# A gated FFT mixer and squared-ReLU MLP, forward and backward: loads of one queue moved to another, and the work around them reordered

## The chip, the cores and the metric

One NeuronCore of a Trainium2 chip. The metric is device time in microseconds (us) of the whole kernel, from its first instruction to its last; the median of three runs is given. A profile is one further execution, taken by the hardware profiler. Its span is a little shorter than the time of the same execution, because something lies before the first and after the last recorded instruction.

The engines, as the profile names them: PE is the matrix engine (PEld its weight loads), DVE the vector engine, ACT the scalar engine, POOL the GpSimd engine, SP the sync engine, which here only issues DMAs. A "q" behind an engine's name (SPq, ACTq) is its sequencer: it waits and issues, while the engine itself may be busy.

## What is computed

The forward function and all its gradients, from a given gradient of the output:

```python
def _A_ref(x, w_r, w_i):                       # x: 1 x 2048 x 1024
    X = rfft2(x.astype(float32), axes=(-2, -1))
    X = X * (w_r + 1j * w_i)                   # w: 2048 x 513
    return irfft2(X, s=(S, D), axes=(-2, -1)).astype(bfloat16)

def _B_ref(x, w1, b1, w2, b2):                 # w1: 1024 x 3584, w2: 3584 x 1024
    h = einsum("bsd,df->bsf", x, w1) + b1
    r = where(h > 0, h, 0)
    return einsum("bsf,fd->bsd", r * r, w2) + b2

g = sigmoid((x * gate_w).sum(-1, keepdims=True))
out = g * _A_ref(x, A_w_r, A_w_i) + (1 - g) * _B_ref(x, B_w1, B_b1, B_w2, B_b2)
# returned: out, and the gradients of x, w_r, w_i, w1, b1, w2, b2, gate_w
```

## The kernel before

The kernel has three stages, one behind the other on PE, and a Fourier transform that runs beside the first two.

**First pass of the MLP** (`mlp_in`, to about 462 us). It computes the hidden layer (`ph`, L740 and L847) and the gradient of the hidden layer (`pd`, L747; DVE makes `dhT` of it on L751), and stores both, transposed, to DRAM (`h2T_scr`, `dhT_scr`). Features go in pairs of 128 (`fp`, 0 to 13), rows in halves (`sp`). A `Unit` is one pair and one half: seven chains of four matmuls (`p1` to `p7`) in place of eight, by Strassen's scheme; between them stand four `back_` steps of the unit before, eight matmuls each. PSUM banks are few: `ph` has two, and `pd` shares two with `pZ`. A `pd` chain starts when DVE has read the bank two chains back. The X bank is copied by ACT (`cu`, `u2`, L851) and then accumulated into again. The sums of rows that the scheme needs lie in the tile `dbn`, whose own contents (gradient rows) have been saved to `db_scr` and are loaded again by `again` (L1001).

**Second pass** (`mlp_grads`, about 462 to 860 us): the gradients of w2 and w1, by `Block`s of seven chains of eight matmuls (L1143). A group of 512 features comes back from DRAM through transposing DMAs (`turned`, L183; four of them make a group) into `even` or `odd` in turn. DVE makes the scheme's sums (`total`, L1075) from these groups and from `dbn`.

**Third pass** (`Outputs`, from about 860 us): the two large outputs.

**The transform.** `fft_mid` is a generator of 32 turns (`turns`: 16 frequency pairs `m`, two halves `h`). A turn loads `z` (two DMAs of 128 KB, L393), adds and subtracts (`mirrored`, L413 and L414), multiplies on PE (`px`, L422), copies to `x` on ACT (L423; an edge column from `ex` on L424), multiplies with the filter on DVE (`products`, L430 and L431), joins to `y` (`joined`, L436 to L442), multiplies back (`pv`, L450; `pc`, L456 and L457), and computes the filter's gradient (`grads_of_w`, L467 to L471). `spread` deals the steps of the transform between the steps of the MLP at a fixed rate, in the first pass 1.5 steps for each step of the MLP. A turn is four steps. The first `px` is at 235.4 us and the last at 595.4 us; their distance repeats as 6.4, 12 and 12 us.

Each engine runs its instructions in the order in which they were recorded. `after(..., NoSync)` fixes an order alone; with `Sync` it is a wait. All hardware-issued DMAs share eight completion semaphores in turn, so a DMA also waits for the landing of the one that used its semaphore last.

SP issues, in one order: the loads of w1 (L769), the transposed loads of w2 and of the groups (L183), the loads of `z` (L393) and of `dbn` (L1001). The two lines that issue what the change moves:

```python
ld(out=z[:, n], in_=columns_of(z_scr, c, h))                       # L393, inputs
after(turned(grp[n][:, k * KH : (k + 1) * KH, f_], in_), later["blocks"])   # fetch
```

In the last units the order of pairs and halves is (11,0), (11,1), (12,0), (12,1), (13,1). The half 0 of pair 13 is done without the scheme, at the very end of the pass (`more`), with `forth` and `back_` in turn and then four `back_` alone.

Of the kernel before, what the change touches and what calls it, by code (L numbers as in the profile page):

```python
# [141 lines left out]
def kernel(  # L142
# [22 lines left out]
    nc = tc.nc  # L165
# [40 lines left out]
    nc.scalar.dma_start(out=identb[:], in_=cten["identb"].ap())  # L206
    kf = pers.tile([P, 2, P], FDT, name="kf", tag="kf")
    flip = pers.tile([P, 1], FP32, name="flip", tag="flip")
# [25 lines left out]
    def columns_of(scr, c, h):  # L234
        return scr[:].rearrange("t c r x h l -> c h (r x) t l")[c, h]
# [89 lines left out]
    def fft_mid(filler):  # L325
        fb, fbs = pool("f2", "right")
        NM, G = R1 // 2, nc.gpsimd
        WL = HW + 2
# [4 lines left out]
        def edges():  # L333

            ed = fb.tile([P, NM, 2, 4], FDT, name="ed", tag="ed")
            low = fb.tile([P, NM, 4], FDT, name="low", tag="low")
            mid = fb.tile([P, 4], FDT, name="mid", tag="mid")
# [19 lines left out]
        def edges_through(ams, ed, low, mid):  # L357
# [8 lines left out]
            for h in range(2):  # L366
                for m in range(NM // 2):
                    for n in range(2):
# [3 lines left out]
                        )  # L372
            ex = fb.tile([P, NM, 2, 2, 2], FDT, name="ex", tag="ex")
            for n in range(2):
                for c in range(2):
                    nc.vector.tensor_copy(
                        out=ex[lanes[n], :, c], in_=sp[lanes[c], :, n, :].rearrange("p m (e t) -> p m t e", e=2)
                    )
            return ex

# [8 lines left out]

        def inputs(m, h):  # L390
            z = fb.tile([P, 2, 2, HW], FDT, name="z", tag="z", bufs=2)
            for n, c in enumerate((m, R1 // 2 + m)):
                ld(out=z[:, n], in_=columns_of(z_scr, c, h))  # L393
            return z
# [22 lines left out]
        def transform(m, h, pm, ex):  # L417
            x = fb.tile([P, 2, 2, WL], FDT, name="x", tag="x", bufs=2)
            px = fps.tile([P, 2, 2, HW], FP32, name="px", tag="ps2", bufs=2)
            for c in range(2):  # L420
                for n in range(2):
                    behind(mm(px[lanes[n], c], lhsT=mats[m][:, 0, n, lanes[c]], rhs=pm[:, n], start=True, stop=True), "PE")  # L422
            nc.scalar.copy(out=x[:, :, :, 0:HW], in_=px[:])  # L423
            nc.scalar.copy(out=x[:, :, :, h * HW], in_=ex[:, m, :, :, h])  # L424
            return x

        def products(h, x, w):
            tt = fb.tile([P, 2, 2, 2, WL], FDT, name="tt", tag="tt")
            W = HW + h
            V(out=tt[:, 0, :, :, 0:W], in0=x[:, :, :, 0:W], in1=w[:, 0:1, 0:W].rearrange("p (o t) l -> p o t l", o=1).to_broadcast([P, 2, 2, W]), op=ALU.mult)  # L430
            V(out=tt[:, 1, :, :, 0:W], in0=x[:, :, :, 0:W], in1=w[:, 1:3, 0:W].rearrange("p (o t) l -> p o t l", o=1).to_broadcast([P, 2, 2, W]), op=ALU.mult)  # L431
# [30 lines left out]
        def grads_of_w(h, x):  # L462
            W = HW + h
            XA, XB = (x[:, :, T, 0:W] for T in range(2))
            gs = fb.tile([P, 2, WL], FDT, name="gs", tag="gs", bufs=2)
            t1_ = fb.tile([P, 2, WL], FDT, name="g1", tag="g1")
            V(out=t1_[:, :, 0:W], in0=XB, in1=XA, op=ALU.mult)  # L467
            V(out=gs[:, 0, 0:W], in0=t1_[:, 0, 0:W], in1=t1_[:, 1, 0:W], op=ALU.add)
            t2_ = fb.tile([P, 2, WL], FDT, name="g1", tag="g1")
# [31 lines left out]
        for u, (m, h) in enumerate(turns):  # L501
            if h:
                eh = fb.tile([P, 2, 2, 2], FDT, name="eh", tag="eh")
            x = transform(m, h, pm, ex)
            yield
# [135 lines left out]

    cf = f1.tile(list(consts["cf"].shape), FDT, name="cf", tag="cf")
    xs = {}

# [62 lines left out]
    def mlp_in():  # L707
# [232 lines left out]
        units_ = [Unit(*u) for u in seq]  # L940
        units_[0].p2()
        for n, u in enumerate(units_):
            fg, pr = divmod(u.fp, NPR)
            if u.sp == 0 and u.fp < LAST:
                load_w1(u.fp + 1)
# [3 lines left out]
            back_(*waiting[0])  # L949
            u.p5()  # L950
            yield
            next(more_sums, None)
            u.p6()
            if n:
                units_[n - 1].square(1, u.copy)
            back_(*waiting[1])
            next(more_sums, None)
            ahead_ = w_sums(u.fp + 1, True) if u.sp == 1 and u.fp < LAST else iter(())
            next(ahead_, None)
            yield  # L960
            u.p7()
            back_(*waiting[2])
            next(more_sums, None)
            next(ahead_, None)
            yield
# [10 lines left out]
            elif n == 2 * DC + 1:  # L976
                grad_of_b2()
            u.p4()
            u.p3()
# [19 lines left out]

    def again(rows_):  # L1000
        ld(out=dbn[:, rows_, :], in_=db_scr[:, rows_, :])  # L1001

# [17 lines left out]
    def mlp_grads():  # L1020
# [8 lines left out]
        def more_of_x(n, last):  # L1029
# [6 lines left out]

        jobs = [(h2T_scr, fg) for fg in range(FG)] + [(dhT_scr, fg) for fg in range(FG)]
        KH, FH = NT // 2, FGW // 2
        grp = {
            n: later["odd" if n % 2 else "even"][:].rearrange("p (t f) -> p t f", t=NT) for n in range(len(jobs))  # L1040
        }

        def fetch(n, *halves):
            if n < len(jobs):
                scr, fg = jobs[n]
                v_ = scr[:].rearrange("c p s -> (c p) s")[fg * FGW : (fg + 1) * FGW, :]
                for i in halves:
                    f_ = slice(i * FH, (i + 1) * FH)
                    for k in range(2):
                        in_ = v_[f_, k * KH * P : (k + 1) * KH * P]  # L1050
                        after(turned(grp[n][:, k * KH : (k + 1) * KH, f_], in_), later["blocks"])
            elif n == len(jobs) and 1 in halves:
                later["block"] = block_of(0)

        fetch(0, 0, 1)

# [785 lines left out]
```

## Time and profile before

| what | us |
|---|---|
| median of three runs | 1209.75 (1209.13 to 1210.87) |
| the profiled execution, its own time | 1206.2 |
| its span | 1204.4 |
| PE busy | 1184.8 (98% of the span) |
| DVE busy | 886.4 (74%) |
| ACT busy | 513.2 (43%) |
| POOL busy | 381.9 (32%) |

The granted clock of PE is 0.999 over the span. Matmuls are pipelined: the profile gives one of 512 columns 0.379 us, but in a chain they start 0.216 us apart (chains of eight start 1.73 us apart). So "busy" PE time overlaps. An idle time that the profile shows is counted from the modelled end of the last matmul, 0.16 us after the next could have started.

### The profile page before, as it was taken

What the parts mean: (1) busy time and instruction counts of PE and PEld (TensorE: products, weight loads), DVE (VectorE), ACT (ScalarE), POOL (GpSimd) and SP (SyncE); (2) the same over time, 40 slices, a digit from 0 to 9 for tenths busy, and PEclk for the clock granted to TensorE, in tenths of its full rate; (3) what the DMA queues carried; (4) which work ended last, traced back from release to release, by engine and by line L of the source; (5) the groups of instructions that cost most, each with busy time, mean ns of one, the idle gap of its engine ahead of it and who ended that gap; (6) DMA issues with size and microseconds to landing.
All of it is one profiled execution on the core that took longest, in us unless ns stands there. A gap on an engine that the chain in (4) does not pass through costs nothing.

```text
span 1204.4 us, 19697 instructions
## 1 busy us (share of the span) xinstructions
PE 1184.8 (98%) x7379; PEld 637.2 (53%) x7379; DVE 886.4 (74%) x1660; ACT 513.2 (43%) x909; POOL 381.9 (32%) x614
## 2 busy tenths in 40 slices
PE   8999999999999998999999999999999999999997
PEld 5565555444344433444446999998544444444444
DVE  3668887589999878777736666666785777977666
ACT  4668888466666663334423566564110110000000
POOL 0223333766666654564341323321001100000000
PEclk9999999999999999999999999999999999999999
DMA  9977575967585899899995999995899999564531
GB/s 287 302 247 227 168 218 159 202 194 202 175 206 177 248 228 246 177 178 230 197 239 126 238 225 250 238 214 161 255 206 273 270 230 273 161 195 144 184 114 36
DMA packets 328986, 249.88 MB, mean 207 GB/s; under 512 B 188200, under 2 KB 287946, under 8 KB 328122
## 3 DMA queue, kind: packets, MB, share of 16 engines
q1 hardware_dynamic: 283808, 119.99, 46.3%
q0 software_dynamic: 35520, 111.74, 29.4%
q10 hardware_dynamic: 9562, 16.89, 4.3%
q8 instruction: 58, 0.95, 0.3%
q14 instruction: 38, 0.31, 0.1%
HBM read 114.84 MB, written 89.67 MB: 170 GB/s over the span
## 4 chain that ended last, share of the span: by engine, by line
PE 74%; DVE 12%; DMA 5%; issue 3%; ACT 3%; SPq 1%; POOL 1%; DVEq 0%; POOLq 0%
PE pX L1143 15%; PE xX L1439 13%; PE pV L1143 11%; PE pd L747 10%; PE xV L1439 7%; PE ph L847 6%; PE xZ L1439 3%; DMA y_scr<-pc 2%; PE ph L740 1%; PE pui L317 1%; PE pki L576 1%; PE pZ L847 1%; PE pu L317 1%; PE px L422 1%; PE pk L286 1%
## 5 line engine op out<-in xcount | busy, mean ns | idle before, releaser
L747 PE MATMUL pd<-dbT,w2T 128*128 128x512 bf16 x896 | 211.0, 379 | 5.0 <-DVE dhT L751 3.9
L747 PEld LDWEIGHTS <-w2T 128*128 128x128 bf16 x896 | 85.7, 98 | 109.9 <-issue 12.3
L1439 PEld LDWEIGHTS <-dS 128*128 128x128 f16 x686 | 66.5, 98 | 78.6 <-issue 3.0
L751 DVE SCALAR_TENSOR_TENSOR dhT<-pd,rT 128x512 bf16<-128x512 f32 x112 | 76.6, 685 | 41.4 <-PE pd L747 39.3
L1490 POOL DMA_DIRECT2D out_dram<-ot x32 | 17.3, 542 | 257.1 <-DVE ot L1546 128.0
L1556 ACT ACTIVATE w2br<-w2br,dsc 128x512 f32<-128x512 bf16 x8 | 5.8, 723 | 172.8 <-DVE ot L1546 117.4
L1439 PE MATMUL xX<-oT,dS 128*128 128x512 f16 x336 | 76.4, 379 | 0.2 <-DVE eR L1468 0.2
L1159 ACT COPY u<-pX 128x512 f32<-128x512 f32 x56 | 32.8, 585 | 93.2 <-PE pX L1143 87.1
L1439 PEld LDWEIGHTS <-odd 128*128 128x128 bf16 (+1 forms) x462 | 44.8, 98 | 51.5 <-issue 0.9
L1439 PEld LDWEIGHTS <-even 128*128 128x128 bf16 (+1 forms) x448 | 43.7, 98 | 52.6 <-issue 0.7
L1143 PEld LDWEIGHTS <-T 128*128 128x128 f16 x672 | 64.4, 98 | 8.2 <-DVE S L1075 1.2
L864 ACT ACTIVATE rT<-rT 128x512 bf16<-128x512 bf16 x69 | 43.3, 628 | 51.2 <-DVE rT L863 51.0
L732 ACT ACTIVATE h2T<-rT 128x1024 bf16<-128x1024 bf16 x56 | 59.7, 1066 | 0.5 <-DMA h2T_scr<-h2T 0.2
L459 POOL DMA_DIRECT2D y_scr<-pc x64 | 47.0, 736 | 36.7 <-DVE pc L456 28.3
L1163 DVE TENSOR_TENSOR whi<-pV,u 128x512 bf16<-128x512 f32 x28 | 19.3, 690 | 51.0 <-ACT u L1159 50.9
L1143 PEld LDWEIGHTS <-S 128*128 128x128 f16 x336 | 31.8, 98 | 43.2 <-DVE S L1075 3.3
L1143 PEld LDWEIGHTS <-resL 128*128 128x128 bf16 x448 | 43.1, 98 | 4.9
L1143 PEld LDWEIGHTS <-resR 128*128 128x128 f16 (+1 forms) x448 | 42.9, 98 | 5.1 <-issue 0.2
L778 POOL DMA_DIRECT2D h2T_scr<-h2T x28 | 20.6, 736 | 73.6 <-ACT f L274 35.7
L232 POOL DMA_DIRECT2D r<-y_scr x48 | 27.9, 584 | 42.8 <-ACT re L555 27.4
L1143 PEld LDWEIGHTS <-even 128*128 128x128 bf16 (+1 forms) x256 | 24.6, 98 | 31.0 <-issue 2.1
L484 POOL DMA_DIRECT2D out_dram<-gw x64 | 34.3, 541 | 17.3 <-ACT gw L480 10.9
(375 smaller groups left out, 2765.3 us busy)
## 6 DMA issues: line engine op xcount, KB each, us to landing
h2T_scr<-h2T POOLq DMA_DIRECT2D x28, 512.0 KB, 4.4
dhT_scr<-dhT POOLq DMA_DIRECT2D x28, 512.0 KB, 5.6
z<-z_scr SPq DMA_DIRECT2D x64, 128.0 KB, 4.1
y_scr<-pc POOLq DMA_DIRECT2D x64, 128.0 KB, 4.2
ax_scr<-yo POOLq DMA_DIRECT2D x16, 512.0 KB, 5.4
out_dram<-ot POOLq DMA_DIRECT2D x31, 256.0 KB, 3.8
out_dram<-whi POOLq DMA_DIRECT2D x28, 256.0 KB, 5.4
out_dram<-wlo POOLq DMA_DIRECT2D x28, 256.0 KB, 4.6
```

The costliest lines, as they stand in the source:

```text
L232: st(out=a, in_=b) if stored else st(out=b, in_=a)
L317: first_ = mm(pu[:, bank, lo : lo + n], lhsT=ft[:, b, :], rhs=mat[:, o : o + n], start=bool(f_ & 1), stop=bool(f_ & 2), skip_group_check=True,
L459: st(out=columns_of(y_scr, c, h), in_=pc[:, n])
L484: st(out=every(dst_w, k), in_=gw[lanes[n], c_, 0:W1])
L732: after(nc.scalar.activation(h2T, rT, ACT.Square), behind_, mybir.DependencyClass.NoSync)
L747: mm(pd[:], lhsT=w_[:, ec, fc % FGC * P : (fc % FGC + 1) * P], rhs=dbT[:, ec, ss], start=(ec == 0), stop=(ec == DC - 1),)
L751: return STT(out=dhT, in0=pd[:], scalar=2.0, in1=rT, op0=ALU.mult, op1=ALU.mult, accum_out=gb1part[:, fc, sb : sb + 1],)
L847: mm(acc[:], lhsT=lhs[:, t, :], rhs=rhs[:, t, :], start=start and t == 0, stop=t == KH - 1, skip_group_check=True)
L864: nc.scalar.activation(rT, rT, ACT.Relu)
L1143: self.mm = mm(out, lhsT=lhs[:, t, m * P : (m + 1) * P], rhs=rhs[:, t, :], start=start and t + a == 0, stop=t == KH - 1, skip_group_check= ...
L1159: turn["ACT"] = nc.scalar.copy(out=t_[:], in_=self.X[:])
L1439: ins = mm(acc, lhsT=lhs[:, fc, :], rhs=rhs[:, fc, :], start=start and fc == 0, stop=fc == KH - 1 and bias is None, skip_group_check=True,)
```

## The change

- The loads of `z` are issued by ACT's queue rather than SP's, behind the copies of `x` (`copied`), one step after `transform` instead of at the end of the turn. The first two stay on SP.
- The `even` group that the second pass reads first is loaded in four pieces in the first pass, one in each of four units (`turned_group(0, ...)`), instead of all four behind the pass's last w1 load. Two of the four loads of the `odd` group are issued later, each behind a chain of the second pass.
- The last units go (11,0), (12,0), (11,1), (12,1), (13,1). `dbn` is loaded again in eight pieces, as rows come free, instead of two halves.
- `x` has three planes: minus the imaginary part, the real, the imaginary. ACT makes the negated plane with one more pass over half of `px`. So `joined` adds once over 1024 columns instead of two operations over 512, and `grads_of_w` takes two operations instead of four. `ex` and `eh` follow suit.
- Small tiles (`ed`, `low`, `mid`) lie in buffers of others, and `kf` moved to another pool.

```diff
-        def inputs(m, h):
+        def inputs(m, h, copied=None):
             z = fb.tile([P, 2, 2, HW], FDT, name="z", tag="z", bufs=2)
             for n, c in enumerate((m, R1 // 2 + m)):
-                ld(out=z[:, n], in_=columns_of(z_scr, c, h))
+                from_ = columns_of(z_scr, c, h)
+                if copied is None:
+                    ld(out=z[:, n], in_=from_)
+                else:
+                    after(nc.scalar.dma_start(out=z[:, n], in_=from_), copied, mybir.DependencyClass.NoSync)
...
-            nc.scalar.copy(out=x[:, :, :, 0:HW], in_=px[:])
+            nc.scalar.copy(out=x[:, 1:3, :, 0:HW], in_=px[:])
+            copied = nc.scalar.mul(out=x[:, 0, :, 0:HW], in_=px[:, 1], mul=-1.0)
             nc.scalar.copy(out=x[:, :, :, h * HW], in_=ex[:, m, :, :, h])
-            return x
+            return x, copied
...
         def joined(h, tt, eh):
+            y = fb.tile([P, 2, 2, HW], FDT, name="y", tag="y")
+            V(out=y[:], in0=tt[:, 0, :, :, 0:HW], in1=tt[:, 1, :, :, 0:HW], op=ALU.add)
             if h:
-                nc.scalar.copy(out=eh[:], in_=tt[:, :, :, :, HW])
+                en = fb.tile([P, 2, 2], FDT, name="en", tag="en")
+                V(out=en[:], in0=tt[:, 0, :, :, HW], in1=tt[:, 1, :, :, HW], op=ALU.add)
+                nc.scalar.mul(out=eh[:, 0], in_=en[:, 1], mul=-1.0)
+                nc.scalar.copy(out=eh[:, 1], in_=en[:, 0])
             else:
-                V(out=tt[:, :, 0, :, 0], in0=tt[:, :, 0, :, 0], in1=eh[:, :, 1, :], op=ALU.subtract)
-                V(out=tt[:, :, 1, :, 0], in0=tt[:, :, 1, :, 0], in1=eh[:, :, 0, :], op=ALU.add)
-            y = fb.tile([P, 2, 2, HW], FDT, name="y", tag="y")
-            V(out=y[:, 0], in0=tt[:, 0, 0, :, 0:HW], in1=tt[:, 1, 1, :, 0:HW], op=ALU.subtract)
-            V(out=y[:, 1], in0=tt[:, 0, 1, :, 0:HW], in1=tt[:, 1, 0, :, 0:HW], op=ALU.add)
+                V(out=y[:, :, :, 0], in0=y[:, :, :, 0], in1=eh[:], op=ALU.add)
...
-            V(out=t1_[:, :, 0:W], in0=XB, in1=XA, op=ALU.mult)
-            V(out=gs[:, 0, 0:W], in0=t1_[:, 0, 0:W], in1=t1_[:, 1, 0:W], op=ALU.add)
-            V(out=t2_[:, :, 0:W], in0=XB, in1=XA[:, ::-1, :], op=ALU.mult)
-            V(out=gs[:, 1, 0:W], in0=t2_[:, 1, 0:W], in1=t2_[:, 0, 0:W], op=ALU.subtract)
+            V(out=t_[:, :, :, 0:W], in0=XB, in1=XA, op=ALU.mult)
+            V(out=gs[:, ::-1, 0:W], in0=t_[:, :, 0, 0:W], in1=t_[:, :, 1, 0:W], op=ALU.add)
...
-        seq = [(fp, sp) for fp in range(2, LAST) for sp in range(2)] + [(LAST, 1)]
+        seq = [(fp, sp) for fp in range(2, LAST - 2) for sp in range(2)]
+        seq += [(fp, sp) for sp in range(2) for fp in (LAST - 2, LAST - 1)] + [(LAST, 1)]
+        freed = seq.index((LAST - 1, 0))
...
+        def freed_rows(n, low, high):
+            if n == freed + 1:
+                again(slice(2 * low, 2 * low + 2), later["last"])
+            elif n == len(seq) - 1 and high:
+                again(slice(6 + 2 * high, 8 + 2 * high))
...
+            if first and u.sp and "mid" in later and u.fp >= FC // 4:
+                turned_group(0, *first.pop(0), later["last"])
...
-            if (u.fp, u.sp) == (LAST - 1, 0):
-                again(slice(0, 8))
-        again(slice(8, NT))
+        again(slice(NT - 2, NT))
...
+    def turned_group(n, i, k, earlier):
+        scr, fg = (h2T_scr, dhT_scr)[n // FG], n % FG
+        rows_ = scr[:].rearrange("c p s -> (c p) s")[fg * FGW + i * FGW // 2 : fg * FGW + (i + 1) * FGW // 2]
+        tiles, f_ = slice(k * NT // 2, (k + 1) * NT // 2), slice(i * FGW // 2, (i + 1) * FGW // 2)
+        after(turned(group(n)[:, tiles, f_], rows_[:, k * S // 2 : (k + 1) * S // 2]), earlier)
...
-        fetch(0, 0, 1)
...
-        fetch(1, 0, 1)
+        fetch(1, 0)
...
+        turned_group(1, 1, 0, blk[1].mm)
...
+        turned_group(1, 1, 1, blk[0].mm)
...
-            x = transform(m, h, pm, ex)
+            x, copied = transform(m, h, pm, ex)
+            if u + 2 < len(turns):
+                z[u + 2] = inputs(*turns[u + 2], copied)
...
-            if u + 2 < len(turns):
-                z[u + 2] = inputs(*turns[u + 2])
```

More of the change, by code (lines that the diff above doesn't have):

```diff
@@ L206 @@
     nc.scalar.dma_start(out=identb[:], in_=cten["identb"].ap())
-    kf = pers.tile([P, 2, P], FDT, name="kf", tag="kf")
     flip = pers.tile([P, 1], FP32, name="flip", tag="flip")
@@ L333, in edges @@
         def edges():
-            ed = fb.tile([P, NM, 2, 4], FDT, name="ed", tag="ed")
-            low = fb.tile([P, NM, 4], FDT, name="low", tag="low")
-            mid = fb.tile([P, 4], FDT, name="mid", tag="mid")
+            ed = fb.tile([P, 2, 2, HW], FDT, name="ed", tag="y")
+            low = fb.tile([P, 2, HW], FP32, name="low", tag="vc")
+            mid = fb.tile([P, 2, 2, HW], FDT, name="mid", tag="pm")
+            flat = lambda t_: t_[:].rearrange("p a b l -> p (a b l)")
+            ed = flat(ed)[:, 0 : NM * 8].rearrange("p (m n e) -> p m n e", n=2, e=4)
+            low = low[:].rearrange("p a l -> p (a l)").bitcast(FDT)[:, 0 : NM * 4].rearrange("p (m e) -> p m e", e=4)
+            mid = flat(mid)[:, 0:4]
             nc.vector.memset(ed[lanes[1], 0], 0.0)
@@ L372, in edges_through @@
                         )
-            ex = fb.tile([P, NM, 2, 2, 2], FDT, name="ex", tag="ex")
+            ex = fb.tile([P, NM, 3, 2, 2], FDT, name="ex", tag="ex")
             for n in range(2):
@@ L376, in edges_through @@
                     nc.vector.tensor_copy(
-                        out=ex[lanes[n], :, c], in_=sp[lanes[c], :, n, :].rearrange("p m (e t) -> p m t e", e=2)
+                        out=ex[lanes[n], :, 1 + c], in_=sp[lanes[c], :, n, :].rearrange("p m (e t) -> p m t e", e=2)
                     )
+            nc.scalar.mul(out=ex[:, :, 0], in_=ex[:, :, 2], mul=-1.0)
             return ex
@@ L417, in transform @@
         def transform(m, h, pm, ex):
-            x = fb.tile([P, 2, 2, WL], FDT, name="x", tag="x", bufs=2)
+            x = fb.tile([P, 3, 2, WL], FDT, name="x", tag="x", bufs=2)
             px = fps.tile([P, 2, 2, HW], FP32, name="px", tag="ps2", bufs=2)
@@ L429, in products @@
             W = HW + h
-            V(out=tt[:, 0, :, :, 0:W], in0=x[:, :, :, 0:W], in1=w[:, 0:1, 0:W].rearrange("p (o t) l -> p o t l", o=1).to_broadcast([P, 2, 2, W]), op=ALU.mult)
-            V(out=tt[:, 1, :, :, 0:W], in0=x[:, :, :, 0:W], in1=w[:, 1:3, 0:W].rearrange("p (o t) l -> p o t l", o=1).to_broadcast([P, 2, 2, W]), op=ALU.mult)
+            for k, (a, b) in enumerate(((1, slice(0, 1)), (0, slice(1, 3)))):
+                by = w[:, b, 0:W].rearrange("p (o t) l -> p o t l", o=1).to_broadcast([P, 2, 2, W])
+                V(out=tt[:, k, :, :, 0:W], in0=x[:, a : a + 2, :, 0:W], in1=by, op=ALU.mult)
             return tt
         def joined(h, tt, eh):
+            y = fb.tile([P, 2, 2, HW], FDT, name="y", tag="y")
+            V(out=y[:], in0=tt[:, 0, :, :, 0:HW], in1=tt[:, 1, :, :, 0:HW], op=ALU.add)
             if h:
-                nc.scalar.copy(out=eh[:], in_=tt[:, :, :, :, HW])
-            else:
-                V(out=tt[:, :, 0, :, 0], in0=tt[:, :, 0, :, 0], in1=eh[:, :, 1, :], op=ALU.subtract)
-                V(out=tt[:, :, 1, :, 0], in0=tt[:, :, 1, :, 0], in1=eh[:, :, 0, :], op=ALU.add)
-            y = fb.tile([P, 2, 2, HW], FDT, name="y", tag="y")
-            V(out=y[:, 0], in0=tt[:, 0, 0, :, 0:HW], in1=tt[:, 1, 1, :, 0:HW], op=ALU.subtract)
-            V(out=y[:, 1], in0=tt[:, 0, 1, :, 0:HW], in1=tt[:, 1, 0, :, 0:HW], op=ALU.add)
+                en = fb.tile([P, 2, 2], FDT, name="en", tag="en")
+                V(out=en[:], in0=tt[:, 0, :, :, HW], in1=tt[:, 1, :, :, HW], op=ALU.add)
+                nc.scalar.mul(out=eh[:, 0], in_=en[:, 1], mul=-1.0)
+                nc.scalar.copy(out=eh[:, 1], in_=en[:, 0])
+            else:
+                V(out=y[:, :, :, 0], in0=y[:, :, :, 0], in1=eh[:], op=ALU.add)
             return y
@@ L463, in grads_of_w @@
             W = HW + h
-            XA, XB = (x[:, :, T, 0:W] for T in range(2))
+            XA, XB = x[:, 0:2, 0, 0:W], x[:, 1:3, 1, 0:W].unsqueeze(1).to_broadcast([P, 2, 2, W])
+            part, *inner = XA.ap
+            XA = bass.AP(tensor=XA.tensor, offset=XA.offset, ap=[part, inner[0], *inner])
             gs = fb.tile([P, 2, WL], FDT, name="gs", tag="gs", bufs=2)
-            t1_ = fb.tile([P, 2, WL], FDT, name="g1", tag="g1")
-            V(out=t1_[:, :, 0:W], in0=XB, in1=XA, op=ALU.mult)
-            V(out=gs[:, 0, 0:W], in0=t1_[:, 0, 0:W], in1=t1_[:, 1, 0:W], op=ALU.add)
-            t2_ = fb.tile([P, 2, WL], FDT, name="g1", tag="g1")
-            V(out=t2_[:, :, 0:W], in0=XB, in1=XA[:, ::-1, :], op=ALU.mult)
-            V(out=gs[:, 1, 0:W], in0=t2_[:, 1, 0:W], in1=t2_[:, 0, 0:W], op=ALU.subtract)
+            t_ = fb.tile([P, 2, 2, 2, WL], FDT, name="g1", tag="tt")[:, 0]
+            V(out=t_[:, :, :, 0:W], in0=XB, in1=XA, op=ALU.mult)
+            V(out=gs[:, ::-1, 0:W], in0=t_[:, :, 0, 0:W], in1=t_[:, :, 1, 0:W], op=ALU.add)
             return gs
@@ L502, in fft_mid @@
             if h:
-                eh = fb.tile([P, 2, 2, 2], FDT, name="eh", tag="eh")
-            x = transform(m, h, pm, ex)
+                eh = fb.tile([P, 2, 2], FDT, name="eh", tag="eh")
+            x, copied = transform(m, h, pm, ex)
+            if u + 2 < len(turns):
+                z[u + 2] = inputs(*turns[u + 2], copied)
             yield
@@ L642 @@
     cf = f1.tile(list(consts["cf"].shape), FDT, name="cf", tag="cf")
+    kf = f1.tile([P, 2, P], FDT, name="kf", tag="kf")
     xs = {}
@@ L937, in mlp_in @@
             pass
-        seq = [(fp, sp) for fp in range(2, LAST) for sp in range(2)] + [(LAST, 1)]
+        seq = [(fp, sp) for fp in range(2, LAST - 2) for sp in range(2)]
+        seq += [(fp, sp) for sp in range(2) for fp in (LAST - 2, LAST - 1)] + [(LAST, 1)]
+        freed = seq.index((LAST - 1, 0))
         more_sums = x_sums(1)
+        def freed_rows(n, low, high):
[3 more added lines that the diff above has]
+                again(slice(6 + 2 * high, 8 + 2 * high))
         units_ = [Unit(*u) for u in seq]
+        first = [(i, k) for i in range(2) for k in range(2)]
         units_[0].p2()
@@ L943, in mlp_in @@
             fg, pr = divmod(u.fp, NPR)
-            if u.sp == 0 and u.fp < LAST:
+            if (u.fp, u.sp) == (LAST - 2, 1):
+                load_w1(LAST)
+            elif u.sp == 0 and u.fp < LAST - 1:
                 load_w1(u.fp + 1)
@@ L950, in mlp_in @@
             u.p5()
+            freed_rows(n, 0, 1)
+            if first and u.sp and "mid" in later and u.fp >= FC // 4:
+                turned_group(0, *first.pop(0), later["last"])
             yield
@@ L953, in mlp_in @@
             u.p6()
+            freed_rows(n, 1, 2)
             if n:
@@ L957, in mlp_in @@
             next(more_sums, None)
-            ahead_ = w_sums(u.fp + 1, True) if u.sp == 1 and u.fp < LAST else iter(())
-            next(ahead_, None)
+            follows = u.fp + 1 if u.sp == 1 and u.fp < LAST - 2 else {(LAST - 2, 0): LAST - 1, (LAST - 1, 1): LAST}.get((u.fp, u.sp))
+            ahead_ = w_sums(follows, True) if follows else iter(())
+            dealt = ahead_ if (u.fp, u.sp) != (LAST - 2, 0) else iter(())
+            next(dealt, None)
             yield
@@ L963, in mlp_in @@
             next(more_sums, None)
-            next(ahead_, None)
+            next(dealt, None)
+            freed_rows(n, 2, 0)
             yield
@@ L978, in mlp_in @@
             u.p4()
+            freed_rows(n, 3, 3)
             u.p3()
@@ L998, in mlp_in, with group, again @@
         xT_s.close()
-    def again(rows_):
-        ld(out=dbn[:, rows_, :], in_=db_scr[:, rows_, :])
+    def group(n):
+        return later["odd" if n % 2 else "even"][:].rearrange("p (t f) -> p t f", t=NT)
+    def turned_group(n, i, k, earlier):
[3 more added lines that the diff above has]
+        after(turned(group(n)[:, tiles, f_], rows_[:, k * S // 2 : (k + 1) * S // 2]), earlier)
+    def again(rows_, earlier=None):
+        after(ld(out=dbn[:, rows_, :], in_=db_scr[:, rows_, :]), earlier)
     def column_sums(sb_pool, acc, tag):
@@ L1035, in more_of_x @@
             loaded[0] = hi
-        jobs = [(h2T_scr, fg) for fg in range(FG)] + [(dhT_scr, fg) for fg in range(FG)]
+        jobs = 2 * FG
         KH, FH = NT // 2, FGW // 2
-        grp = {
-            n: later["odd" if n % 2 else "even"][:].rearrange("p (t f) -> p t f", t=NT) for n in range(len(jobs))
-        }
+        grp = {n: group(n) for n in range(jobs)}
         def fetch(n, *halves):
-            if n < len(jobs):
-                scr, fg = jobs[n]
-                v_ = scr[:].rearrange("c p s -> (c p) s")[fg * FGW : (fg + 1) * FGW, :]
+            if n < jobs:
                 for i in halves:
-                    f_ = slice(i * FH, (i + 1) * FH)
                     for k in range(2):
-                        in_ = v_[f_, k * KH * P : (k + 1) * KH * P]
-                        after(turned(grp[n][:, k * KH : (k + 1) * KH, f_], in_), later["blocks"])
-            elif n == len(jobs) and 1 in halves:
+                        turned_group(n, i, k, later["blocks"])
+            elif n == jobs and 1 in halves:
                 later["block"] = block_of(0)
-        fetch(0, 0, 1)
         def sums_of_b1():
```

## The prediction

> **What bounds the kernel now.** I read the page first. PE is busy for 98% of the span at clock 0.999, so only PE's own gaps can be won.
>
> ```profile
> PE 1184.8 (98%) x7379; PEld 637.2 (53%) x7379; DVE 886.4 (74%) x1660; ACT 513.2 (43%) x909; POOL 381.9 (32%) x614
> ```
>
> Second, PE's waits, longest in total first: what it waits for, us in total, times, the longest.
>
> ```profile
> PE pd L747 <- DVE dhT L751: 3.9, 2, 3.3
> PE pX L1143 <- DVE S L1075: 1.6, 3, 0.7
> ...
> PE pd L747 <- DVE rT L863: 1.1, 3, 0.6
> ```
>
> The largest sits in two places at the end of the first pass. The timeline of PE there, and of DVE just before:
>
> ```profile
> 447.69 1.90 PE L740 MATMUL ph<-xT,w1g 128*128 128x512 bf16 x8
> 450.24 3.61 PE L747 MATMUL pd<-dbT,w2T 128*128 128x512 bf16 x16 [0.65 <-DVE dhT L751]
> 457.13 5.34 PE L747 MATMUL pd<-dbT,w2T 128*128 128x512 bf16 x24 [3.27 <-DVE dhT L751]
> ```
>
> ```profile
> 439.75 0.08 DVE L751 DVE_READ_ACCUMULATOR dhT<-pd,rT 128x1 f32 x1
> 445.20 0.43 DVE L413 TENSOR_TENSOR pm<-z 128x512 f16<-128x512 f16 x1 [5.36 <-DMA z<-z_scr]
> ```
>
> DVE stands still for 5.36 us, because `z` has not landed; what queues behind it, the `dhT` that frees a `pd` bank among it, comes late, up to 456.39. The lost PE time, start to start: the chain from 447.69 ends its starts at 447.69 + 1.73 = 449.42 and the next begins at 450.24, 0.82 lost; 16 matmuls later 450.24 + 3.46 = 453.70, the next at 457.13, 3.43 lost; together 4.25 us. Why `z` is late is in SP's timeline:
>
> ```profile
> 414.68 1.96 SPq L393 DMA_DIRECT2D z<-z_scr  x2
> 416.68 21.53 SPq L183 DMA_TRANSPOSE even<-h2T_scr  x3
> 438.31 2.60 SPq L393 DMA_DIRECT2D z<-z_scr  x4
> ```
>
> Three transposed loads held SP's queue for 21.5 us; the four `z` loads behind them went out at 438.31. How close DVE runs to its limit shows in the busy time by stage (PE, PEld, DVE, ACT, POOL): 102 of 110 us in the first stretch.
>
> ```profile
> 235.00:345.00 110.00, 109.23 (x554) 44.90 (x553) 102.06 (x244) 72.80 (x123) 71.24 (x114) 1.00 0.68 196
> 450.00:463.00 13.00, 9.48 (x45) 3.97 (x45) 8.63 (x25) 3.55 (x7) 8.39 (x14) 1.00 1.13 279
> ```
>
> **The `z` loads on ACT.** Before, a pair on SP takes 0.36 + 0.47 us to issue and lands in 4.1 us (median; 2.1 to 12.1). On ACT no transposed load stands ahead of it. After turn u's copies the pair for turn u + 2 goes out some 2 us behind `px`, and `pm` needs it some 2.5 us behind the next `px`, so it has 6.5 us at the short distance of 6.4 and 12 at the others. So the 5.36 us wait goes, and with it the 4.25 us of PE: in the new order DVE has only the two `pm`, two `tt` and the `dhT` between 447 and the end of the pass. Bounds: 0, if `z` lands as late as 12.1 us, to 4.25. I take 4.25, since only 6.2 us of all DVE time is charged to `z`, all of it beside those transposes.
>
> A rule speaks against this: the Trainium skill, DMA: Bandwidth & Descriptors, section "Issuing engines are not separate DMA queues", says that DMAs of all queues interleave on the same 16 engines and that another issuer saves only issuing time. The `z` pair that went out at 445.99 beside dense traffic would be its case. By the rule alone, were transfers the limit, this term would be near 0; by the row of SP above it was issuing time that was lost, and the term stays.
>
> What ACT takes on, per turn: one pass over 512 columns out of PSUM (nearest row: `vc`, L455, 0.58 us, 0.48 start to start) and the issue of two DMAs, 0.83 us. The issue can hide: at 860.56 ACT's queue issues a DMA while its engine is in an activation from 860.55 to 861.61. So 0.5 us at least and 1.3 at most. Behind it in ACT's order wait the copies that free the X bank. The tightest is `u2`: at 319.81 `px`, 320.90 `p6`, and `p7` at 323.50 needs `u2`. Before, ACT runs `x` 320.47, `vc` 321.38, `gw` 321.86 (1.1 us), `u2` 322.87 to 323.45: just in time. After, the order is `x`, the negated plane, both `z`, `vc`, `u2`, and `gw` behind it: `x` 320.47, plane 321.38, 321.86 (issue hidden) to 322.69 (not), `vc` 0.48, `u2` 0.57, so ready between 322.9 and 323.75. The loss is 0 to 0.25 us, in one turn of three, 7 times: 0 to 1.8. I take 0.4, nearer the overlap that the row shows. At the other two places of the pattern the spare time is larger (308.15 `px`: `cu` ready at 312.2, needed at 313.67).
>
> Waits of the pair itself: it shares completion semaphores with SP's loads, so ACT stands if such a load has not landed. The closest is the pair placed at 559, behind a transposed load that SP issues at 545: 14 us, against 5.9 to 10.3 for landings there. Cost 0; if that cover went, the join's copies on ACT and the `pV` banks behind them would come late by as much.
>
> **The negated plane on DVE.** Per turn `y` falls from two operations (0.34 each, start to start) to one of 1024 columns; nearest row `tt`, 1028 columns, 0.60: 0.08 saved. `g`, `gs`, `g`, `gs` take 1.55 us (511.90 to 513.45, their bubbles included); one of 1024 (0.60), a bubble 0.11 and one of 512 (0.34) make 1.05: 0.5 saved. The edges even out. So 0.55 to 0.6 us a turn. DVE is not the bound, so this is worth only what PE waits for it in the first pass: `rT`, 1.1 us idle and three times the 0.16 that the modelled end hides, 1.6 us. The three stand at 276, 306 and 396, behind `pc` and `y` in a backlog that shrinks by 0.55 a turn, and against it stands ACT's later `x`. Bounds 0 to 1.6; I take 1.1.
>
> **What this shifts to.** In the new order of DVE, the last turn of the first pass has its `y`, the edge, `g` and `gs` behind the last `dhT`, ahead of the sums for the second pass. Before, `g` and `gs` had been done during PE's stall. From the last `dhT` (463.19) DVE took 10.36 us to the second sum `S` (end 473.55): `y` 0.67, `pc` 1.20, `T` 2.20, `S` 1.14, `wlo` 0.60, `even` 1.13, `T` 2.20, `S` 1.22. Now `y` takes 0.60, the edge 0.07, `g` and `gs` 1.05: 1.05 more. PE, that waited 0.83 us there (start to start), waits 1.9: 1.05 lost. Bounds 0 (if the gap before the last `dhT` takes them) to 1.05; the order says 1.05.
>
> **Loads dealt out.** I cost these at nothing, with this cover. `even`, four loads at 259 to 349: first read at 462.94. `dbn`, eight pieces at 395 to 436: first read at 465.06, 29 us behind the last, where a half landed in 9.9 us; without the cover the sum `T` waits. w1 of pair 12 goes out at 359 and is first read at 375, that of pair 13 at 405 and 415, against landings of 4.3 to 9.2 us. `odd`: its third and fourth load go out at about 466 and 472 in the new time; DVE reads the last at about 482, PE needs the sum at 488, and DVE takes 3.1 us from the one to the other; landings there were 8.4 to 12.4. So up to 2.5 us behind its place costs nothing. Beyond that `pX` of group 1 waits.
>
> **Sum.** 4.25 - 1.05 + 1.1 - 0.4 = 3.9 us. By this sum the profiled execution goes from 1206.2 to 1202.3. It lies 3.55 below the median of the runs, its span 1.8 below its own time; both stay, so the median goes from 1209.75 to 1205.85.
>
> **Rivals.**
> (1) DVE takes the gain back at the second pass's start: its chain of sums sets the start of `p6`, whatever PE wins before. For it: DVE is busy 33.66 of 37 us from 463 to 500. Against: the chain starts with the last `dhT`, which moves with PE. Should `odd` land late as well (2.5 us), 1.4 us are left: 1208.3, no change.
> (2) Slower: ACT's queue. The place is `u2` before `p7`. If one of the two issues takes 1.67 us, the longest that an issue of `z` took on SP, and the other its 0.47, `u2` is ready at 321.86 + 2.14 + 0.48 + 0.57 = 325.05, PE loses 1.55 us, 7 times: 10.9, against 4.25 - 1.05 + 1.1 = 4.3 won: 1209.75 + 6.6 = 1216.3. It decides from 0.6 us a time (4.3 / 7). Against: SP's median was 0.47, and the long ones stood among transposes on the same queue.
> (3) Slower: `z` lands late beside the transposed loads now dealt to 259, 289, 319 and 349, each just ahead of the short distance. At 12.1 us instead of 6.5 DVE stands 5.6 us, as before 450, and PE loses 4.25 each time, 17 at most; with one or two of four 1209.75 - 3.9 + 6.4 = 1212. Against: at 292.21 a `z` beside two transposes landed in 4.3 us.
> (4) The change doesn't do what it says: `z` at 438 is as late for want of transfer (the stage's DMA share is 1.13). Only `rT` is won: about 1209.
>
> **How the numbers follow.** Mine 0.62, (1) 0.15, (2) 0.09, (3) 0.08, (4) 0.06. My own case runs from 4.25 + 1.6 = 5.85 won (1203.9) to 4.25 - 1.05 - 1.8 = 1.4 (1208.4). Below it the waits for `S` in the second pass (1.6 us) could shrink too: 1202.5. Above, half of (2) and (3) is taken in: 1211.5. What a measurement here can tell from no change is 0.2%, 2.4 us: below 1207.3 faster, above 1212.2 slower. Most of my case (0.58 of 0.62) and a part of (1) and (4) are faster: 0.66. No change: the rest of these and half of (3): 0.20. Slower: (2) and the rest of (3): 0.14.
>
> **What would show it.** Right: DVE's idle time before `pm` for a DMA is gone, PE runs from 447 to the second pass without a wait above 0.3 us, `S` in the first blocks costs some 1.9 us, 96 DVE instructions are missing (three a turn), ACT is busier by some 20 us (32 x 0.58 and the small edge copies). Wrong: `ph` waits for ACT's `u2` or `cu` in rows above 0.3 us; DVE waits for `z` at 267, 298, 328 or 358; PE waits for `odd`.

## The result and the profile after

| | before | changed |
|---|---|---|
| median | 1209.44 (6 runs) | 1204.49 (1203.54 to 1206.71, 6 runs) |
| ratio, 95% interval | | 0.9957 (0.994 to 0.9975) |
| profiled execution: its time, its span | 1206.2, 1204.4 | 1203.54, 1201.8 |

Some executions, of every kernel, fall in a slower state of the chip (one of these six of before, 1239.39): ratios leave them out, medians and ranges do not.

The kernel is faster by some 5 us in the medians, but only by 2.7 us between the two profiled executions: the one of before, 1206.2, was shorter than any of the six. The busy time of the changed kernel, from its page:

```profile
PE 1185.0 (99%) x7379; PEld 637.8 (53%) x7379; DVE 873.4 (73%) x1564; ACT 532.9 (44%) x958; POOL 381.9 (32%) x614
```

DVE has 96 instructions and 13.0 us less, ACT 19.7 us more. The end of the first pass and the start of the second in PE's timeline:

```profile
447.82 0.62 PE L430 MATMUL px<-pm,ab 128*64 128x512 f16 x4
448.38 1.90 PE L751 MATMUL ph<-xT,w1g 128*128 128x512 bf16 x8
450.12 8.80 PE L758 MATMUL pd<-dbT,w2T 128*128 128x512 bf16 x40
458.85 0.60 PE L461 MATMUL pv<-y,ab 64*128 64x512 f16 x4
...
467.78 1.90 PE L1173 MATMUL pV<-T,even 128*128 128x512 f16 x8 [0.23 <-DVE even L1105]
471.12 1.90 PE L1173 MATMUL pX<-T,S 128*128 128x512 f16 x8 [1.44 <-DVE S L1105]
```

Forty `pd` matmuls run without a gap where before PE stood twice, 4.25 us in all. In exchange the two first blocks wait longer for DVE's sums. The same place before:

```profile
470.51 0.61 PE L450 MATMUL pv<-y,ab 64*128 64x512 f16 x4
471.05 1.90 PE L1143 MATMUL pV<-T,even 128*128 128x512 f16 x8
473.61 1.90 PE L1143 MATMUL pX<-T,S 128*128 128x512 f16 x8 [0.67 <-DVE S L1075]
```

Before, `pV` starts 0.54 us behind `pv`, without a wait, and `pX` 2.56 us behind `pV`, of which 1.73 are the chain: 0.83 us lost. In the changed kernel `pv` starts at 466.95 and `pV` 0.83 us behind it (0.29 lost), and `pX` waits 1.60 us more (1.44 and 0.16 that the modelled end hides): 1.89 us in all, 1.06 more than before. PE's waits in the changed kernel by sum, in us, times and longest:

```profile
PE pX L1173 <- DVE S L1105: 1.9, 2, 1.4
PE pd L758 <- DVE rT L874: 1.8, 1, 1.8
```

The three `rT` waits of before (at 276, 306 and 396) are gone, but one new one is longer than the three together. It and its cause, in PE's, DVE's, SP's and ACT's timelines:

```profile
248.22 1.89 PE L758 MATMUL pd<-dbT,w2T 128*128 128x512 bf16 x8 [1.78 <-DVE rT L874]
```

```profile
247.08 0.42 DVE L421 TENSOR_TENSOR pm<-z 128x512 f16<-128x512 f16 x1 [2.85 <-DMA z<-z_scr]
247.42 0.74 DVE L874 SCALAR_TENSOR_TENSOR rT<-pZ,b1col,cu 128x512 bf16<-128x512 f32 x1
```

```profile
225.40 11.39 SPq L183 DMA_TRANSPOSE w2T<-in_B_w_dram  x2
```

```profile
236.69 1.32 ACTq L401 DMA_DIRECT2D z<-z_scr  x2
```

`pm` stands ahead of the `rT` that PE needs, and waits for a `z` pair that went out on the heels of two transposed loads of w2. Before, the wait was there too (0.82 us), but `rT` stood ahead of `pm`: one of the `g` operations that are now merged filled that place. DVE before:

```profile
243.57 0.42 DVE L467 TENSOR_TENSOR g<-x 128x514 f16<-128x514 f16 x1
243.90 0.74 DVE L863 SCALAR_TENSOR_TENSOR rT<-pZ,b1col,cu 128x512 bf16<-128x512 f32 x1
246.95 0.81 DVE L413 TENSOR_TENSOR pm<-z 128x512 f16<-128x512 f16 x1 [0.82 <-DMA z<-z_scr]
```

### The profile page after: what moved, and what is told of

Same layout as the page of the kernel before. It is cut to its first block, busy times and chain, and to the rows that moved or that the text cites. A ratio compares the mean times of both kernels' runs of the same rounds, so it can differ in the third digit from the quotient of the medians.

```text
span 1201.8 us, 19680 instructions
## 1 busy us (share of the span) xinstructions
PE 1185.0 (99%) x7379; PEld 637.8 (53%) x7379; DVE 873.4 (73%) x1564; ACT 532.9 (44%) x958; POOL 381.9 (32%) x614
## 4 chain that ended last, share of the span: by engine, by line
PE 82%; DVE 7%; DMA 4%; issue 2%; ACT 2%; SPq 1%; POOL 1%; DVEq 0%; POOLq 0%
PE pX L1173 15%; PE xX L1471 13%; PE pd L758 13%; PE pV L1173 11%; PE ph L858 8%; PE xV L1471 7%; PE xZ L1471 3%; PE ph L751 2%; PE pui L316 1%; PE pv L461 1%; PE px L430 1%; PE pZ L858 1%; PE pki L586 1%; PE pu L316 1%; PE pk L285 1%
## 5 line engine op out<-in xcount | busy, mean ns | idle before, releaser
L441 DVE TENSOR_TENSOR tt<-x,w 128x1028 f16<-128x1028 f16 (+1 forms) x64 | 41.5, 689 | 14.1 <-issue 10.4
```

Source lines behind the costliest of these rows:

```text
L441: V(out=tt[:, k, :, :, 0:W], in0=x[:, a : a + 2, :, 0:W], in1=by, op=ALU.mult)
```

## Experiments

All ratios are to the kernel before, on the same chip, with a 95% interval. The twelve kernels ran in three sets of four, each set on another chip; between sets the ratios are compared.

**Each part by itself.** Four kernels: `z` on ACT alone; the negated plane alone; the loads dealt out, the order of the last units and the `dbn` pieces alone; and the changed kernel with `z` back on SP.

```diff
 # z_on_act: the kernel before, with
+            x, copied = transform(m, h, pm, ex)
+                z[u + 2] = inputs(*turns[u + 2], copied)        # nc.scalar.dma_start, behind copied
 # plane_only: the kernel before, with ex, transform, products, joined and grads_of_w of the changed one
 # dealt_only: the changed kernel, with those five and inputs of the one before
 # z_on_sp: the changed kernel, with
-                z[u + 2] = inputs(*turns[u + 2], copied)
+                z[u + 2] = inputs(*turns[u + 2])                # nc.sync.dma_start, at the end of the turn
```

> The kernel before, with the z loads alone moved to ACT, issued behind the turn's copy of px. My theory (SP's queue was blocked by three transposed loads, so the issuing time was lost): DVE's wait before pm for a DMA near 445, 5.36 us, is gone, and with it up to 4.25 us of PE. The last g and gs stand ahead of the last five dhT in DVE's order, 1.55 us that the stall hid before, so I expect 3 us, about 1206.4. The three rT waits (1.6 us) stay, and no wait appears near 246, since pm still stands behind rT there. Rival (the z transfers themselves are slow in that stage): the wait before pm stays above 3 us and the time stays within 1 us of 1209.4.

> The kernel before, with the negated plane alone (z on SP, the turned loads together, the old order of units and two db loads). My theory: the 4.25 us at the end of the first pass stay, the three rT waits go (-1.6 us), the last turn's g and gs now stand ahead of the sums S (+1.26 us), ACT's later copies cost 0.36 us, and the new pd wait for rT near 246 is there as in the changed kernel (+1.95 us), because the plane's DVE order puts pm ahead of rT there and z lands late whoever issues it. Sum +2.0 us, about 1211.4. Rival A (the wait near 246 comes from issuing z on ACT): no wait there, about 1209.4. Rival B (cheaper turns are worth all of DVE's saving, 13 us of busy time): below 1207.

> The kernel before, with the dealt-out turned loads, the order of the last units and the db reload in eight pieces alone; z stays on SP at its old place. Theory one (what blocked z was the three transposed loads at 416 to 438, so moving them away is enough): DVE's 5.36 us wait before pm near 445 is gone, PE wins about 3 us there; against that the four places where a transposed piece now goes out (near 259, 289, 319, 349) may hold z on SP by some 7 us each, up to 4 x 4.25. Without loss there about 1206.4. Theory two, mine on record (ACT's issue is what wins): the stall moves to those four places, PE loses at least 3 us in all there, and the time is 1209.4 or more.

> The changed kernel with the z loads back on SP at their old place, all else kept. If ACT's issue is what wins: DVE waits for z behind the dealt transposed pieces at 267, 298, 328 and 358, over 2 us each, PE loses 3 us or more and the time is 1207.5 or more. If dealing the transposed loads out is enough: no such waits, and the time is that of the changed kernel, 1204.5, or a few tenths less for ACT's spared issues. The pd wait for rT near 246 (1.95 us) stays in both, if it comes from DVE's order and not from ACT.

| kernel | median | ratio, interval |
|---|---|---|
| z_on_act | 1214.96 | 1.0034 (1.0018 to 1.0051) |
| plane_only | 1209.12 | 0.9979 (0.9961 to 0.9998) |
| dealt_only | 1203.48 | 0.9943 (0.9926 to 0.996) |
| z_on_sp | 1205.61 | 0.9952 (0.9934 to 0.997) |

My theory fell with the first: ACT alone makes the kernel slower, where the theory had 1206.4 and its rival no change. The profile is of the slowest of its ten runs (1222.84), so its waits may be longer than those of a median run. In its DVE timeline the waits for `z` are there, two of three longer than the 5.36 us of before:

```profile
435.57 0.42 DVE L417 TENSOR_TENSOR pm<-z 128x512 f16<-128x512 f16 x1 [2.53 <-DMA z<-z_scr]
453.11 0.42 DVE L417 TENSOR_TENSOR pm<-z 128x512 f16<-128x512 f16 x1 [8.29 <-DMA z<-z_scr]
466.34 0.43 DVE L417 TENSOR_TENSOR pm<-z 128x512 f16<-128x512 f16 x1 [6.96 <-DMA z<-z_scr]
```

ACT issued in time; the data came late. The row of four transposed loads on SP, the issue of the pair that DVE had at 453.11 on ACT, and the loads issued from 432 to 446 us with their median time to landing (last column), from the view of DMAs:

```profile
407.36 37.30 SPq L183 DMA_TRANSPOSE even<-h2T_scr  x4
```

```profile
432.85 0.37 ACTq L397 DMA_DIRECT2D z<-z_scr  x1
433.82 0.37 ACTq L397 DMA_DIRECT2D z<-z_scr  x1
```

```profile
z<-z_scr ACTq DMA_DIRECT2D x3, 128.0 KB, 19.1
even<-h2T_scr SPq DMA_TRANSPOSE x2, 19.8
```

Beside the row of transposed loads a `z` load that ACT issues takes 19.1 us. In the changed kernel the `z` loads issued from 440 to 451 us, with a single transposed load issued behind them (of `odd`, at 450.31), take:

```profile
z<-z_scr ACTq DMA_DIRECT2D x4, 128.0 KB, 5.2
odd<-h2T_scr SPq DMA_TRANSPOSE x1, 4.9
```

With the loads dealt out and `z` on SP the whole gain is there (dealt_only, 3 us below the 1206.4 expected), and with everything else but ACT's issue too (z_on_sp): both intervals hold the changed kernel's 0.9957. z_on_sp has no DVE wait for `z` behind the dealt pieces, and it has the `rT` wait near 246, as has plane_only: DVE's order makes it, not ACT. The two waits, z_on_sp first, and plane_only's loss at the end of the pass:

```profile
248.83 1.89 PE L758 MATMUL pd<-dbT,w2T 128*128 128x512 bf16 x8 [2.73 <-DVE rT L874]
```

```profile
250.30 1.89 PE L754 MATMUL pd<-dbT,w2T 128*128 128x512 bf16 x8 [3.09 <-DVE rT L870]
457.98 5.34 PE L754 MATMUL pd<-dbT,w2T 128*128 128x512 bf16 x23 [1.19 <-DVE dhT L758]
```

plane_only missed its 1211.4: DVE still waited 4.38 us for `z` at 447.95, but with less work queued behind it PE lost 1.35 us there (the 1.19 and the 0.16 that the modelled end hides) instead of 4.25. I had not counted that.

**Which of the dealt loads.** The changed kernel with the four `even` loads together again; and the kernel before with nothing but these four dealt out.

```diff
 # even_together: the changed kernel, with
-                turned_group(0, *first.pop(0), later["last"])
+        fetch(0, 0, 1)                                          # mlp_grads, as before
 # even_only: the kernel before, with
+            if first and u.sp and "mid" in later and u.fp >= FC // 4:
+                turned_group(0, *first.pop(0), later["last"])
-        fetch(0, 0, 1)
```

> The changed kernel with the four transposed loads of even back together at their old place; z stays on ACT. If the transposed loads' transfers hold z (what z_on_act showed: z from ACT landed after 9 to 19 us beside them): z pairs at the end of the first pass land after 12 us or more, DVE waits before pm for a DMA by over 4 us there, and the time is 1210 or more, although nothing stands ahead of z on ACT's queue. If issuing on SP was the limit, as my prediction had it: no such wait, and 1204.5 as the changed kernel.

> The kernel before, with the four transposed loads of even dealt out alone; z on SP, old order of the last units, db in two pieces, no negated plane. If dealing them out is the whole gain: no wait of DVE before pm above 1 us at the end of the first pass, z lands in 4 to 8 us, and the time is 1204 to 1205.5. If the order of the last units and the db pieces are needed too (the db halves beside the z loads): z still lands after 8 us and the time is 1207 or more.

even_together: 1221.37, ratio 1.0088 (1.0062 to 1.0114). even_only: 1202.31, ratio 0.9932 (0.9911 to 0.9953). So the four `even` loads carry the whole gain, and alone they win more than expected (1204 to 1205.5). In even_only one such load by itself holds SP for 2.56 us (first row), PE keeps one short wait at the end of the pass, and the `z` loads from SP at 439 to 450 us land in 7.7 us:

```profile
259.33 2.56 SPq L183 DMA_TRANSPOSE even<-h2T_scr  x1
```

```profile
452.57 5.34 PE L747 MATMUL pd<-dbT,w2T 128*128 128x512 bf16 x23 [0.50 <-DVE dhT L751]
```

```profile
z<-z_scr SPq DMA_DIRECT2D x4, 128.0 KB, 7.7
```

In even_together DVE waits 4.55 us for `z`, as expected, and a second mechanism shows, in DVE's and ACT's timelines:

```profile
416.28 0.42 DVE L421 TENSOR_TENSOR pm<-z 128x512 f16<-128x512 f16 x1 [4.55 <-DMA z<-z_scr]
```

```profile
413.36 0.60 ACT L432 ACTIVATE x<-px 128x512 f16<-128x512 f32 x1
425.88 0.40 ACTq L401 DMA_DIRECT2D z<-z_scr  x1
426.32 0.22 ACT L433 COPY x<-ex 128x6 f16<-128x6 f16 x1 [12.35 <-DMA even<-h2T_scr]
```

Here ACT could not even issue: the `z` load waited for the landing of an `even` load (the trace has both on completion semaphore 115), and ACT stood 12.35 us with all its copies behind it. PE paid at once:

```profile
429.55 1.86 PE L858 MATMUL ph<-xT,Sw 128*128 128x512 f16 x4 [13.69 <-ACT u L862]
```

So most of even_together's loss is this stall of ACT; what the late landing of `z` alone would have cost there is not shown.

**The two new waits.** Two ties in DVE's order, on the changed kernel (both) and with `z` on SP (both_sp):

```diff
+            after(first_, earlier, mybir.DependencyClass.NoSync)    # pm of turn 2, both operations, behind the last rT
+            after(V(out=t_[:, :, :, 0:W], in0=XB, in1=XA, op=ALU.mult), earlier, mybir.DependencyClass.NoSync)  # turn 21, behind S
```

> The changed kernel with two ties in DVE's order: the first pm behind the rT that it had overtaken near 246, and the last first-pass turn's g and gs behind the second sum S. My reading of the two waits: the pd wait for rT near 246 (1.95 us start to start) falls below 0.4, the two waits for even and S at the start of the second pass fall from 2.09 to 0.85 us, and the time is 1204.5 - 1.6 - 1.2 = 1201.7. Rival (DVE is short of time there, so what is pushed back is missed next): the rT wait returns at one of the next turns, or pV for wlo and the next S waits by over 1 us, and the time stays within 1 us of 1204.5.

> As the run before, with the z loads back on SP at their old place. If the issuer of z is worth nothing: 1201.7 within 1 us, and no wait of DVE before pm above 1 us at the four places of the dealt pieces. If ACT's issue is worth something once the other two waits are gone: 1203 or more.

The expectations of both and plane_only reckon with 2.09 us for `even` and `S`, 1.26 more than before; by the rows it is 1.89, 1.06 more. both: 1201.03, ratio 0.9917 (0.9894 to 0.9941), against the 1201.7 expected. both_sp: 1201.97, ratio 0.9928 (0.9907 to 0.9948). The rival, that DVE is short of time there, falls. ACT's issue is worth about 1 us in the medians, which the intervals can't tell from nothing.

**Place, number, and what is needed.** On one chip: the changed kernel again; `even` dealt out with the plane and the two ties, the rest as before (even_plane); `even` in two pairs (even_pairs); all four in a row at the first place (even_early).

```diff
 # even_pairs, even_early: even_only, with
-                turned_group(0, *first.pop(0), later["last"])
+                for _ in range(2):                              # even_early: while first:
+                    turned_group(0, *first.pop(0), later["last"])
```

> The changed kernel itself, beside the next three on one chip, so that they can be compared with it. Its ratio to the kernel before should fall within 0.994 and 0.9975 again. If the pieces beyond the dealing out of even cost something (the wait for rT near 246 and the later S sums, 3.2 us in its profile), it is slower than the two kernels that deal even out without them by 1.5 us or more.

> The kernel before, with even dealt out, the negated plane and the two ties in DVE's order; z on SP, old order of the last units, db in two pieces. If z on ACT, the order of the last units and the db pieces are worth nothing: the time is that of the kernel with all of them and both ties, 1201 to 1202, and a few tenths below even dealt out alone. If the db half that goes out at 435 still hurts (0.66 us of PE for dhT at 451.7 when even alone was dealt out): 1202.5 or more.

> Even dealt out alone, but in two pairs of transposed loads at the first two places instead of four single ones. If what holds z is the number of transposed loads that follow each other: the z pair behind a pair goes out and lands some 5 us later than behind a single one (SP takes 2.5 us for one alone, and 6 to 9 us for one behind another), DVE waits for z by 1 to 4 us at one or both places, and the time is 1203 to 1206. If four in a row are needed: as with single ones, 1202.3.

> Even dealt out alone, but all four transposed loads in a row at the first place, near 259. If a row of four is what holds z, wherever it stands: the stall moves there, SP is held for some 20 us, DVE waits before pm by 4 us or more, and the gain over the kernel before is gone (1207 or more). If what was wrong was the place at the end of the pass (the db reload and w1 beside it): no stall, about 1202.3.

| kernel | median | range | ratio, interval |
|---|---|---|---|
| changed_again | 1204.5 | 1203.12 to 1207.5 | 0.9957 (0.994 to 0.9974) |
| even_plane | 1201.53 | 1201.27 to 1202.98 | 0.9928 (0.9905 to 0.9952) |
| even_pairs | 1203.2 | 1202.16 to 1232.46 | 0.9946 (0.9927 to 0.9964) |
| even_early | 1205.23 | 1203.45 to 1218.69 | 0.997 (0.9946 to 0.9993) |

A row of four moves the stall to its new place. SP's and DVE's timelines of even_early:

```profile
261.48 17.61 SPq L183 DMA_TRANSPOSE even<-h2T_scr  x4
279.20 2.05 SPq L393 DMA_DIRECT2D z<-z_scr  x4
```

```profile
285.24 0.42 DVE L413 TENSOR_TENSOR pm<-z 128x512 f16<-128x512 f16 x1 [5.26 <-DMA z<-z_scr]
```

SP is held 17.61 us, some seven times the 2.56 of a single load, and DVE stands 5.26 us, nearly the 5.36 of before. But the kernel keeps part of the gain, so the place at the pass's end was worse than this one; 1207 was too much. Two in a row cost no wait for `z`: the expected 1 to 4 us did not come, and 1203.2 is at the lower end of what I gave.

even_plane does without ACT's issue, the order of the last units and the eight `dbn` pieces, and is as fast as both_sp. Its runs and those of changed_again, 3 us slower in the median, do not overlap; against even_pairs changed_again is 1.3 us slower, where I had expected 1.5 or more. So the rest of the change, without the ties, cost more than it won. Even the plane with its two ties adds nothing that these runs can tell: even_only alone had 0.9932. even_plane's PE timeline at the two places, and what it still waits for `rT`:

```profile
246.10 1.89 PE L758 MATMUL pd<-dbT,w2T 128*128 128x512 bf16 x8
...
468.76 1.90 PE L1165 MATMUL pX<-T,S 128*128 128x512 f16 x8 [0.67 <-DVE S L1097]
```

```profile
PE pd L758 <- DVE rT L874: 0.8, 2, 0.5
```

No wait near 246, two shorter ones for `rT` elsewhere, and 0.83 us, start to start, for `S`.

## Why the prediction was right, and where it was not

The time was right (1205.8 against 1204.49), the side too. The main term had the right size and the wrong cause. By the terms as they turned out the sum was 2.85 and not 3.9, and the 5 us of the medians hold a part that is not explained: that prediction and median came out so near is in part luck.

- **"It was issuing time that was lost, and the term stays"** is the step that failed. The stall went, all 4.25 us, but not because ACT issued `z`: ACT alone gave +0.34%. The row of SP was read rightly, `z` did go out late; but the time spared by issuing on ACT came back as time to landing, 19.1 us beside the row of transposed loads. A row of before pointed there: the four `z` loads that SP issued from 445.99 on took 11.3 us in the median. That SP itself was held by their transfers is my reading of the rows (2.56 us for one, 17.61 for four in a row). The rule that I set aside held: the Trainium skill, DMA: Bandwidth & Descriptors, section "Issuing engines are not separate DMA queues", says that another issuer saves issuing time alone. z_on_act agrees: the load that ACT issued at 433.82 landed 19.2 us later.
- **"Loads dealt out. I cost these at nothing"**: right as a cost, but this edit carries the gain (even_only, 0.9932). I had asked only whether `even` still comes in time, not what its going away leaves free.
- **S sums, -1.05**: 1.06 (1.89 against 0.83). Right in place, mechanism and size; the tie takes it back.
- **`rT`, +1.1**: all three waits went (1.6), and the new one near 246 took 1.94 (1.78 and the 0.16 that the modelled end hides). No term of the sum had it: I read DVE's new order at the end of the pass and not at its first turn, where a `z` was already late: of the 6.2 us that DVE waited for `z` before, which I put beside the `even` loads, 0.82 stood at 246.95, behind the loads of w2.
- **ACT, -0.4**: no row of `u2` or `cu` above 0.3 us in the changed kernel's profile; the profile of changed_again has one, `cu` at 369.18, of 0.61 (0.77 start to start). With `z` on ACT or on SP the medians differ by about 1 us.
- **ACT's semaphore wait, cost 0 under its cover**: the cover held. even_together shows the price without it, 12.35 us.
- **Rivals.** (1) and (2) did not come. (3) needed `z` late beside single dealt pieces: not even `z` on SP is. (4), that `z` was late for want of transfer, was right in its mechanism and wrong in its time, because dealing the loads out took the row away.
- **The sum.** 3.9 predicted, 2.7 between the profiled executions (4.25 + 1.6 - 1.06 - 1.94 = 2.85 by the terms above), 5 in the medians. The last gap is not settled: no profile of a median run of before was taken. Of the 27 runs of before beside changed_again, the 10 with a granted clock below 0.997 took 1212.9 us on average, the other 17 took 1209.0; the changed kernel's ten lay at 0.996 to 0.999.

## What to carry to other kernels

When a small load is late behind large ones in a queue, ask first whether the queue or the transfer holds it: issue it elsewhere, alone, and read its time to landing. If that grows, thin out the large loads: a single one of `even` between the small ones cost nothing here, two in a row neither, two of w2 held the `pm` behind them for 2.85 us, and four of `even` in a row made a stall at each of the three places where they stood. And when instructions are merged, read the new order at every place where a wait was only just hidden.

## What was not expected of the hardware

The granted clock falls in a long stall of PE, and stays down for some microseconds behind it. Stretches of even_together (busy us of PE, PEld, DVE, ACT, POOL; then the clock, the DMA share and GB/s):

```profile
405.00:415.00 10.00, 9.95 (x49) 4.18 (x49) 5.32 (x11) 6.23 (x11) 4.59 (x8) 1.00 1.10 184
415.00:420.00 5.00, 0.86 (x5) 0.29 (x3) 0.76 (x2) 0.00 (x0) 0.53 (x1) 0.83 1.20 204
420.00:425.00 5.00, 0.00 (x0) 0.00 (x0) 0.00 (x0) 0.00 (x0) 0.00 (x0) 0.50 1.29 156
425.00:430.00 5.00, 0.45 (x2) 0.17 (x2) 2.25 (x4) 1.79 (x4) 1.48 (x2) 0.50 0.99 331
430.00:435.00 5.00, 5.00 (x15) 1.44 (x13) 1.90 (x6) 2.13 (x4) 4.40 (x7) 0.50 1.11 364
435.00:440.00 5.00, 5.00 (x26) 2.00 (x24) 5.00 (x15) 2.72 (x5) 0.74 (x1) 0.96 0.51 162
```

PE stands for 13.7 us; from 430 to 435 it works again, at half the clock, and starts 15 matmuls where 26 follow in the next 5 us. So a long stall costs more than its own length; the 3.4 us stall in the profile of before left the clock at 1.00.
